# Attention scores of one head at a time, keys split over the two row halves of the array

## The chip, the cores and the metric

The kernel runs on one core of a Trainium2 chip. The metric is the device time of one launch in microseconds (us), from the first to the last instruction with what lies around them; the table below has the median of three runs.

## What is computed

Attention with a bias that a small network computes from positions, and a mixture of two experts out of eight on its result:

```
scores = q @ k.T / 8 + bias[h, i, j]        # B=4, H=8, S=576, D=64
attn   = exp(scores - max) / (sum + 1e-9)
x      = (attn @ v) as 2304 tokens x 512
noisy  = x @ w_gate + log1p(exp(x @ w_noise)) * noise
out    = sum over the top 2 experts: weight * relu(x @ w1[e]) @ w2[e]   # 8 experts, 512 -> 1024 -> 512
```

The bias is relu(psi * w1 + b1) @ w2 with psi = log1p|i-j| / log1p(max(i,1)); it is the same for all batches.

## The kernel before

The program has three stages. First the **bias stage** writes the bias of all heads (36 blocks; `bias_ops`: relus on VectorE and ScalarE at L341 and L344, products at L352, evacuation to a tile X at L360 and L362, a DMA into the bias tiles). Then the **attention stage** runs 16 units, each a batch and a pair of heads, with the routing of a finished batch (`route_ops`) between units. Last the **expert stage** runs the experts (L905, L934); it takes over half of the time and isn't touched.

A unit has four tiles of 128 queries and one (t = 4) that holds the last 64 queries of both heads: nine score tiles of 128 x 576. For each (`pair_ops`):

- *scores*: products on TensorE (PE) into a PSUM tile D of two banks, 288 keys in each (`fqk`, L448). q and k are split into a high and a low part (QH, QL, KH, KL) and three products are summed. The operands' 64 channels fill half of the array's rows; two products in two row halves run side by side. Before, head 0 lies in the upper half and head 1 in the lower, so the two heads of a pair run together and both D tiles must be free. For t = 4 the two heads' queries are stacked with zeros beside them and go through the full array, six products of 128 rows.
- *bias and maximum*: one VectorE instruction per head reads D and the bias and writes a tile E of 128 x 640 (L457, `fttr`); a small copy (L470, `cp`) moves the last 64 keys of head 0 beside those of head 1.
- *exponentials* on ScalarE in place (L463, `fexp`), which also sum up the row.
- *turning*: transposes on PE from E to a D tile, 8 for head 0 and 10 for head 1 (`fturn`, L478), also in row halves, and an evacuation of 512 or 640 columns into ET by VectorE or ScalarE (`evac_op`, L424, L426).
- *values*: ET times v in column halves, 256 or 320 wide, per two or three tiles (`av_ops`, L514), 20 instructions in the trace, and its evacuation into R.

Each unit's q and k are loaded (SyncE's queue, SP) into raw tiles, the high part is cast on VectorE or ScalarE (`fhi`, L405 and L407), and the low part is a subtraction on GpSimd or VectorE (`flo`, L410), a unit ahead, into one of two sets of QH, QL, KH, KL.

The order of everything up to the expert stage is made when the program is built: `Sched` holds operations with a wanted time (`pr`, from constants such as `STEP`, `PO`, `AVO`), costs in a planner's model, dependencies and rings of buffers (`rings`: four D, eight E, two ET, three VT), and puts each on an engine in the order in which it could start. Engines then run their rows in that order and wait for each other by semaphores. Routing has its own operations in the same order: gate products, turned results, token rows to DRAM (x, L707 and L717), ranks, and scatters of slots by GpSimd (L687); after the routing of batch 2 the first tokens of the experts are gathered (L853) and transposed (L871) between the last attention work.

Of the kernel before, what the change touches and what calls it, by code (L numbers as in the profile page):

```python
# [6 lines left out]
F32 = mybir.dt.float32  # L7
# [10 lines left out]
HP = H // 2  # L18
# [3 lines left out]
QW = (EW, S)  # L22
# [46 lines left out]
class Sched:  # L69
# [112 lines left out]
DRAIN, WEIGHTS = 0.18, 0.1  # L182


def build(tc, qs, ks, vp, pe_w1, pe_b1, pe_w2, gate, noise, w1, w2, out):
# [111 lines left out]
    def tw_rest(e):  # L297
# [90 lines left out]
    def unit_ops(u, pr):  # L388
# [4 lines left out]
        for j in (1, 0):  # L393
            if u:
                raw = Buf(f"Q{j}")
                ld = [sd.add(pr - QO[1] + 4 * (1 - j), [[("SP", 0.06), ("DMA", 1.64)]],
                             lambda e, j=j, raw=raw: sy.dma_start(raw.t, (qs, ks)[j][b, hp]), [], [raw], f"ld{u}.{j}")]
            else:
                raw, ld = Buf(f"Q{j}"), []
                raw.slot, raw.t, rings[f"Q{j}"].slots[0] = 0, raws[u, j], None  # L400
# [10 lines left out]
            q = pr - QO[0] + (0.5 if j == 0 else 0)  # L411
# [9 lines left out]
    def evac_op(pr, w, o, i, deps, bufs, kind):  # L421
# [5 lines left out]
        a, d = {640: (0.68, 0.8), 512: (0.55, 0.65), 256: (0.264, 0.331), 128: (0.2, 0.198), 64: (0.17, 0.131)}[w]  # L427
# [4 lines left out]
    def pair_ops(n):  # L432
# [764 lines left out]
```

## Time and profile before

| what | value |
|---|---|
| median of three runs | 764.07 us (763.04 to 764.13) |
| the profiled execution | 764.54 us, of which the span of its instructions is 762.8 us |
| granted TensorE clock over the span | 0.995 |
| PE (matmul) busy | 729.0 us, 96% |
| PE weight loads (PEld) busy | 598.2 us, 78% |
| VectorE (DVE) busy | 472.2 us, 62% |
| ScalarE (ACT) busy | 412.2 us, 54% |
| GpSimd (POOL) busy | 222.4 us, 29% |

The bias stage's last product starts in the 71st microsecond, the attention's last value product ends at about 303 us, and the expert stage fills the rest. A line of the page or of an answer names the line of the code, the engine, the operation, out<-in by the names of the tiles, and times. Busy time of PE is modelled from the starts of matmuls, which are pipelined, so it contains short stalls.

### The profile page before, as it was taken

To read this page: it belongs to the slowest core of one execution; us is meant where nothing else is said; L and a number is where in the kernel's file an instruction comes from. 1 tells how busy PE (TensorE), PEld (TensorE's weight loads), DVE (VectorE), ACT (ScalarE), POOL (GpSimd) and SP (SyncE) were. 2 spreads that over 40 slices of the span, in tenths; PEclk is the share of its full clock that TensorE was granted. 3 is DMA by queue.
4 is the path that set the end of the run, shared out by engine and by line. 5 is a ranking of instruction groups with operands and counts; after the bars stand their busy time and mean duration, and the time that the engine had idled before them with its cause. 6 is when DMAs were issued, how large, how long until landed. Compare 5 with 4: busy or idle time off the path is not lost.

```text
span 762.8 us, 16211 instructions
## 1 busy us (share of the span) xinstructions
PE 729.0 (96%) x6289; PEld 598.2 (78%) x6289; DVE 472.2 (62%) x1104; ACT 412.2 (54%) x815; POOL 222.4 (29%) x229
## 2 busy tenths in 40 slices
PE   6889999999999999999999999999999999999993
PEld 3455677777777775889999899899889889999982
DVE  8898678978977976666543474435344444453361
ACT  8999778897897887334422263332333323333230
POOL 2200122332241242745140435226035034032031
PEclk9999999999999999999999999999999999999998
DMA  5857543432342314458552576355155245345140
GB/s 149 211 160 206 178 149 108 131 90 69 108 91 69 107 23 160 173 145 292 170 202 65 191 240 199 121 169 201 64 172 189 97 153 176 110 138 185 56 143 22
DMA packets 45990, 108.38 MB, mean 142 GB/s; under 512 B 10509, under 2 KB 15373, under 8 KB 45904
## 3 DMA queue, kind: packets, MB, share of 16 engines
q1 hardware_dynamic: 35520, 77.58, 33.5%
q0 software_dynamic: 10384, 29.67, 11.9%
q8 instruction: 52, 0.85, 0.5%
q14 instruction: 34, 0.28, 0.1%
HBM read 77.54 MB, written 19.38 MB: 127 GB/s over the span
## 4 chain that ended last, share of the span: by engine, by line
PE 82%; DVE 10%; ACT 3%; DMA 2%; issue 2%; POOLq 0%; POOL 0%; SPq 0%; DVEq 0%; ACTq 0%
PE Y L934 28%; PE Ha L905 14%; PE Hb L905 14%; PE D L514 9%; PE D L448 7%; PE D L478 4%; PE D L352 3%; DMA bias<-X 2%; DVE E L457 2%; DVE ET L426 2%; PE XT L871 1%; DVE X L717 1%; ACT E L463 1%; DVE lz L627 1%; ACT R L341 1%
## 5 line engine op out<-in xcount | busy, mean ns | idle before, releaser
L934 PE MATMUL Y<-wh,hh 128*128 128x512 f32 x608 | 199.8, 393 | 0.4 <-DVE hh L911 0.3
L934 PEld LDWEIGHTS Y<-wh,hh 128*128 128x128 f32 x608 | 112.8, 186 | 23.6 <-DVE hh L911 0.9
L934 PE MATMUL Y<-wl,hh 128*128 128x512 f32 (+2 forms) x320 | 125.5, 392 | 0.0
L463 ACT ACTIVATE E<-E,mxt 128x576 f32<-128x576 f32 x144 | 110.4, 770 | 7.2 <-DVE mxt L457 6.4
L831 DVE TENSOR_TENSOR wl<-wr,wh 128x1024 fp32r<-128x1024 f32 x77 | 95.4, 1240 | 28.3 <-ACT wh L829 28.2
L457 DVE CUSTOM_DVE_ANT_0 E<-D,bias 128x576 f32<-128x576 f32 x128 | 92.4, 753 | 11.7 <-PE D L448 11.3
L907 ACT ACTIVATE hh<-Ha 128x300 fp32r<-128x300 f32 (+5 forms) x64 | 26.8, 419 | 131.1 <-PE Ha L905 112.5
L514 PE MATMUL D<-ET,vt 128*64 128x256 f32 (+1 forms) x640 | 85.2, 411 | 0.0
L829 ACT ACTIVATE wh<-wr 128x1024 fp32r<-128x1024 f32 x80 | 84.0, 1052 | 1.5 <-DMA wr<-in_w_dram 1.5
L911 DVE SCALAR_TENSOR_TENSOR hh<-Ha,hh 128x128 fp32r<-128x128 f32 (+5 forms) x72 | 30.4, 432 | 84.4 <-ACT hh L907 84.1
L905 PE MATMUL Ha<-xh,wh 128*128 128x300 f32 (+5 forms) x256 | 79.6, 311 | 0.0
L905 PE MATMUL Ha<-xh,wl 128*128 128x300 f32 (+5 forms) x256 | 77.5, 303 | 0.0
L905 PE MATMUL Ha<-xl,wh 128*128 128x300 f32 (+5 forms) x256 | 77.4, 302 | 0.0
L478 PEld LDWEIGHTS D<-identr,E 64*128 64x128 f32 x1312 | 53.8, 138 | 28.6 <-ACT E L463 14.9
L905 PE MATMUL Hb<-xh,wh 128*128 128x300 f32 (+5 forms) x248 | 75.2, 303 | 0.0
L905 PE MATMUL Hb<-xh,wl 128*128 128x300 f32 (+5 forms) x248 | 74.6, 301 | 0.0
L905 PE MATMUL Hb<-xl,wh 128*128 128x300 f32 (+5 forms) x248 | 74.5, 301 | 0.0
L448 PE MATMUL D<-KH,QH 64*128 64x288 f32 (+1 forms) x288 | 70.1, 340 | 4.3 <-DVE mxt L457 2.0
L424 ACT ACTIVATE ET<-D 128x512 f32<-128x512 f32 (+2 forms) x125 | 66.6, 538 | 12.3 <-PE D L478 5.5
L946 POOL DMA_INDIRECT out_dram<-y,ixt x40 | 46.0, 1151 | 86.6 <-DVE y L939 80.6
L478 PE MATMUL D<-identr,E 64*128 64x64 f32 x1312 | 64.9, 229 | 5.9 <-ACT E L463 1.8
L911 DVE SCALAR_TENSOR_TENSOR hh<-Hb,hh 128x224 fp32r<-128x224 f32 (+5 forms) x86 | 30.3, 376 | 62.3 <-ACT hh L907 62.0
(193 smaller groups left out, 1395.4 us busy)
## 6 DMA issues: line engine op xcount, KB each, us to landing
wr<-in_w_dram SPq DMA_DIRECT2D x80, 512.0 KB, 4.6
bias<-X SPq DMA_DIRECT2D x32, 288.0 KB, 3.9
raw<-in_qs_dram SPq DMA_DIRECT2D x16, 320.0 KB, 3.2
vt<-in_vp_dram SPq DMA_DIRECT2D x16, 320.0 KB, 3.4
raw<-in_ks_dram SPq DMA_DIRECT2D x16, 288.0 KB, 3.0
out_dram<-gmz SPq DMA_DIRECT2D x18, 256.0 KB, 3.4
xs_scratch<-X SPq DMA_DIRECT2D x16, 256.0 KB, 2.9
biasr<-X SPq DMA_DIRECT2D x8, 144.0 KB, 2.5
```

What stands on the lines that cost most here:

```text
L424: sc.activation(o(), i(), AF.Copy)
L448: te.matmul(SS[s].t[:, h, :SH], qb.t[x][r, cs], qb.t[y][r, ks], start=(i == 0), stop=(i == 2), skip_group_check=True)
L457: dv.tensor_tensor_reduce(EE[s].t[:, :S].rearrange("p (a b) -> p a b", a=2), SS[s].t[:, :, :SH], bt.rearrange("p (a b) -> p a b", a=2), op ...
L463: sc.activation(EE[s].t[:, :S], EE[s].t[:, :S], AF.Exp, bias=mx[s], scale=-1.0, accum_out=col)
L478: te.transpose(PP[s].t[:, r.start // 64, 64 * k:64 * k + 64], EE[s].t[r, c0:c0 + 128], ident[r, r])
L514: te.matmul(o.t[64 * s:64 * s + 64, 0, :w], vt.t[:, k0, 64 * s:64 * s + 64], et.t[:, 4 * s + k0 if k0 < 4 else 8, :w], start=(k0 == 0), st ...
L829: sc.activation(wh[:, cs], r[:, cs], AF.Copy)
L831: eng.tensor_tensor(wl[:, cs], r[:, cs], wh[:, cs].bitcast(F32), op=OP.subtract)
L905: te.matmul(p[:, :w], a[:, o:o + 128], x[it][:, d, cs], start=(i == 0), stop=(i == 11))
L911: dv.scalar_tensor_tensor(o, p[:, i:i + n], 0.0, HH[:, c0 + i:c0 + i + n].bitcast(F32), op0=OP.max, op1=OP.subtract)
L934: te.matmul(Y if fold else Y[:m], h, w[:, o:o + 512], start=(f == 0 and i == 0), stop=(f == NFC - 1 and i == len(terms) - 1))
L946: st = gp.indirect_dma_start(out=out, out_offset=bass.IndirectOffsetOnAxis(ap=IX[it][:m, 1, k:k + 1], axis=0), in_=y[:m], in_offset=None, ...
```

## The change

Scores are now made for one head at a time. Each head's queries are held in both row halves (`qs` has an array per head, the 64 channels twice), and its keys are split over them: the upper half takes keys 0 to 287, the lower half keys 288 to 575, into the two banks of one D tile. An operation `qk` is six products of one head instead of twelve of two, and needs one free D tile. For t = 4 the two heads' six products each are summed into one D tile, with zeros in the queries of the other head; nothing of the scores goes through the full array. There are two q arrays to load, cast and subtract in each unit instead of one; the E ring has five tiles instead of eight, VT two instead of three, X five instead of four. The planner's costs and wanted times are changed throughout (a price between row products and row transposes, `TURN`, among them), so the order of all engines up to the expert stage is new.

```diff
-QW = (EW, S)
-            c += DRAIN if op.form != self.form else WEIGHTS if t > self.free[e] + WEIGHTS else 0.0
+            c += TURN.get(self.form + op.form, DRAIN) if op.form != self.form else WEIGHTS if t > self.free[e] + WEIGHTS else 0.0
...
-T0, TE, STEP = 15.737, 4.119, 1.527
+T0, TE, STEP = 28.874, 3.875, 1.28
...
+TURN = dict(rowrowt=0.05, rowtrow=0.1)
...
-    for j in (1, 0):
+    for j in (2, 0, 1):
...
-        E=Ring(8, lambda k: (wk if k < 5 else wq).tile([128, EW], F32, name=f"E{k}", bufs=1)),
+        E=Ring(5, lambda k: wk.tile([128, EW], F32, name=f"E{k}", bufs=1)),
...
-        VT=Ring(3, lambda k: wk.tile([128, 5, 128], F32, name=f"vt{k}", bufs=1)),
-        Q0=Ring(1, lambda k: wq.tile([128, EW], F32, name="raw0", bufs=1)),
-        Q1=Ring(1, lambda k: wq.tile([128, S], F32, name="raw1", bufs=1)),
-        QK=Ring(2, lambda k: [wq.tile([128, QW[x[0] == "K"]], F32R, name=f"{x}{k}", bufs=1)
-                                for x in ("QH", "QL", "KH", "KL")]),
+        VT=Ring(2, lambda k: wk.tile([128, 5, 128], F32, name=f"vt{k}", bufs=1)),
+        Q=Ring(2, lambda k: wq.tile([128, EW], F32, name=f"raw{k}", bufs=1)),
+        K=Ring(1, lambda k: wq.tile([128, S], F32, name="raw2", bufs=1)),
+        QK=Ring(2, lambda k: [wq.tile([128, S if x[0] == "K" else EW], F32R, name=f"{x}{k}", bufs=1)
+                              for x in ("QH0_", "QL0_", "QH1_", "QL1_", "KH", "KL")]),
...
-        a, d = {640: (0.68, 0.8), 512: (0.55, 0.65), 256: (0.264, 0.331), 128: (0.2, 0.198), 64: (0.17, 0.131)}[w]
+        a, d = {640: (0.585, 0.735), 512: (0.49, 0.6), 256: (0.27, 0.341), 64: (0.17, 0.131)}[w]
...
-        def fqk(e):
-            for h in range(2):
-                ks = slice(h * SH, h * SH + SH)
-                for i, (x, y) in enumerate(((0, 2), (0, 3), (1, 2))):
-                    for s in range(ns):
-                        r, cs = (HALF[s], slice(128 * t, 128 * t + 128)) if t < 4 else (slice(0, 128), slice(512, EW))
-                        te.matmul(SS[s].t[:, h, :SH], qb.t[x][r, cs], qb.t[y][r, ks], start=(i == 0), stop=(i == 2),
-                                  skip_group_check=True)
-        q = sd.add(pr, ("PE", 0.82), fqk, PREP[u] + QKOP[-1:], [qb] + SS, f"qk{n}", "row" if t < 4 else "full")
+        def fqk(s):
+            def f(e):
+                for h in ((s,) if t < 4 else (0, 1)):
+                    for i, (x, y) in enumerate(((0, 4), (0, 5), (1, 4))):
+                        for r in range(2):
+                            te.matmul(SS[s].t[:, r, :SH], qb.t[2 * h + x][HALF[r], 128 * t:128 * t + 128],
+                                      qb.t[y][HALF[r], h * SH:h * SH + SH], start=(i == 0 and (t < 4 or h == 0)),
+                                      stop=(i == 2 and (t < 4 or h == 1)), skip_group_check=True)
+            return f
+        for s in range(ns):
+            qs_.append(sd.add(pr + STEP * s, ("PE", 0.395 if t < 4 else 0.79), fqk(s), PREP[u][:2 + s if t < 4 else 3] + QKOP[-1:],
+                              [qb, SS[s]], f"qk{n}.{s}", "row"))
...
-    qs = np.zeros((B, HP, 2 * D, EW), f)
+    qs = np.zeros((B, HP, 2, 2, D, EW), f)
+    ks = np.zeros((B, HP, 2, D, 2, SH), f)
```

How the order changes is shown at three places.

**PE, the scores of the last 64 queries in a unit soon after the bias stage.** L448 (before) and L450 (after) are scores from KH, KL and QH, QL, L478 and L485 are transposes of an E tile; a number behind a name tells the buffer. Before:

```order
L478 MATMUL D3_1956<-identr_140,E6_1898 128x64 x8
L478 MATMUL D2_1968<-identr_140,E7_1907 128x64 x10
L448 MATMUL D1_1987<-KH0_1655,QH0_1653 128x288
L448 MATMUL D1_1987<-KL0_1656,QH0_1653 128x288
L448 MATMUL D1_1987<-KH0_1655,QL0_1654 128x288
L448 MATMUL D1_1987<-KH0_1655,QH0_1653 128x288
L448 MATMUL D1_1987<-KL0_1656,QH0_1653 128x288
L448 MATMUL D1_1987<-KH0_1655,QL0_1654 128x288
L478 MATMUL D3_1996<-identr_140,E0_1965 128x64 x8
```

After, where x2 is the two row halves, and QH0 and QH1 are the two heads:

```order
L485 MATMUL D3_2013<-identr_142,E3_1929 128x64 x8
L450 MATMUL D1_2026<-KH0_1686,QH0_0_1682 128x288 x2
L450 MATMUL D1_2026<-KL0_1687,QH0_0_1682 128x288 x2
L450 MATMUL D1_2026<-KH0_1686,QL0_0_1683 128x288 x2
L450 MATMUL D1_2026<-KH0_1686,QH1_0_1684 128x288 x2
L450 MATMUL D1_2026<-KL0_1687,QH1_0_1684 128x288 x2
L450 MATMUL D1_2026<-KH0_1686,QL1_0_1685 128x288 x2
L485 MATMUL D2_2045<-identr_142,E4_1953 128x64 x10
L450 MATMUL D0_2060<-KH0_1686,QH0_0_1682 128x288 x2
L450 MATMUL D0_2060<-KL0_1687,QH0_0_1682 128x288 x2
L450 MATMUL D0_2060<-KH0_1686,QL0_0_1683 128x288 x2
L485 MATMUL D3_2068<-identr_142,E0_2000 128x64 x8
```

The 18 transposes of two heads that followed each other before, and the scores of a whole pair, are now cut into turns of one head's scores and one head's transposes; t = 4 is twelve half products (the six rows on D1_2026) instead of six full ones. The transposes that follow a head's scores belong, here as in nearly all of the program, to the head three before it.

**ACT in the same part of the program.** L463 and L470 are exponentials, L424 and L427 evacuations into ET (turned exponentials) and R (values), L407 a cast. Before:

```order
L407 ACTIVATE KH1_1903<-raw1_1688 128x576
L463 ACTIVATE E6_1898,SM_542<-E6_1898,mxt_1899 128x576
L463 ACTIVATE E7_1907,SM_542<-E7_1907,mxt_1908 128x576
L424 ACTIVATE R0_1934<-D0_1886 128x256
L424 ACTIVATE ET0_1838<-D3_1913 128x4x128
L424 ACTIVATE ET1_1979<-D3_1956 128x4x128
L463 ACTIVATE E0_1965,SM_542<-E0_1965,mxt_1966 128x576
L463 ACTIVATE E1_1981,SM_542<-E1_1981,mxt_1982 128x576
L424 ACTIVATE ET1_1979<-D3_1996 128x4x128
L463 ACTIVATE E2_2006,SM_542<-E2_2006,mxt_2007 128x576
L463 ACTIVATE E3_2037,SM_542<-E3_2037,mxt_2038 128x576
```

After:

```order
L470 ACTIVATE E1_1884,SM_405<-E1_1884,mxt_1885 128x576
L427 ACTIVATE ET0_1894<-D1_1918 128x5x128
L470 ACTIVATE E2_1905,SM_405<-E2_1905,mxt_1906 128x576
L470 ACTIVATE E3_1929,SM_1134<-E3_1929,mxt_1930 128x576
L427 ACTIVATE R0_1968<-D0_1940 128x256
L427 ACTIVATE ET0_1894<-D3_1970 128x4x128
L470 ACTIVATE E4_1953,SM_1134<-E4_1953,mxt_1954 128x576
L427 ACTIVATE ET0_1894<-D2_1987 128x5x128
L427 ACTIVATE ET1_2039<-D3_2013 128x4x128
L470 ACTIVATE E0_2000,SM_1134<-E0_2000,mxt_2001 128x576
L427 ACTIVATE ET1_2039<-D2_2045 128x5x128
```

Evacuations of 640 columns (128x5x128), of which VectorE has 25 of 64 before, all but one stand on ACT now, between the exponentials.

**PE at the end of the attention.** L514 and L520 are the last value products, L871 and L877 the transposes of the experts' first tokens, which need gathered rows xg. Before:

```order
L478 MATMUL D0_5318<-identr_140,E4_5266 128x64 x8
L871 MATMUL Y0_5388<-identr_140,xg_5361 128x128 x4
L478 MATMUL D1_5393<-identr_140,E2_5269 128x64 x10
L514 MATMUL D0_5405<-ET1_5211,vt0_4748 64x256 x10
L478 MATMUL D1_5423<-identr_140,E3_5327 128x64 x8
L871 MATMUL Y1_5434<-identr_140,xg_5361 128x128 x4
L478 MATMUL D0_5442<-identr_140,E1_5331 128x64 x10
L871 MATMUL Y2_5454<-identr_140,xg_5361 128x128 x4
L514 MATMUL D1_5462<-ET0_5314,vt0_4748 64x320 x10
```

After:

```order
L485 MATMUL D1_5511<-identr_142,E2_5458 128x64 x8
L520 MATMUL D0_5579<-ET1_5367,vt1_5190 64x256 x10
L485 MATMUL D1_5592<-identr_142,E4_5461 128x64 x10
L485 MATMUL D0_5605<-identr_142,E0_5499 128x64 x8
L877 MATMUL Y0_5618<-identr_142,xg_5552 128x128 x4
L877 MATMUL Y1_5626<-identr_142,xg_5552 128x128 x4
L877 MATMUL Y2_5631<-identr_142,xg_5552 128x128 x4
L485 MATMUL D1_5638<-identr_142,E1_5520 128x64 x10
L520 MATMUL D0_5657<-ET0_5509,vt1_5190 64x320 x10
```

The three groups of token transposes, spread between the last heads before, stand in one piece now, ahead of the last head's transposes and its value product.

## Rows read from the trace of the kernel before

**Rows 1.** The page, part 1: busy us, share of the span, instructions.

```profile
PE 729.0 (96%) x6289; PEld 598.2 (78%) x6289; DVE 472.2 (62%) x1104; ACT 412.2 (54%) x815; POOL 222.4 (29%) x229
```

**Rows 2.** Two stretches: length, busy us by engine, PE clock, DMA share, GB/s.

```profile
0.00:71.00 71.00, 59.41 (x718) 31.48 (x718) 66.01 (x166) 66.72 (x107) 9.67 (x22) 1.00 0.68 180
71.00:303.00 232.00, 223.26 (x2915) 165.63 (x2913) 185.54 (x565) 191.32 (x455) 66.55 (x57) 1.00 0.37 108
```

**Rows 3.** The chain that ended last, 100 to 300 us: start, us, what.

```profile
154.81 2.84 PE D L514 x20
169.13 2.84 PE D L514 x20
...
182.94 2.87 PE D L514 x20
200.28 2.87 PE D L514 x20
```

**Rows 4.** The timeline from 164 us: start, us, engine, line, [idle before <-releaser].

```profile
163.42 1.56 POOL L410 TENSOR_TENSOR QL<-raw,QH 128x640 fp32r<-128x640 f32 x1
...
164.19 0.78 PE L478 MATMUL D<-identr,E 64*128 64x64 f32 x18
...
164.77 0.41 PE L448 MATMUL D<-KH,QH 64*128 64x288 f32 x2
...
164.99 0.32 PE L448 MATMUL D<-KL,QH 64*128 64x288 f32 x2
...
165.51 0.33 PE L448 MATMUL D<-KH,QL 64*128 64x288 f32 x2
...
165.65 0.82 PE L478 MATMUL D<-identr,E 64*128 64x64 f32 x18
165.84 0.76 DVE L457 CUSTOM_DVE_ANT_0 E<-D,bias 128x576 f32<-128x576 f32 x1 [0.81 <-PE D L448]
...
166.66 0.40 PE L448 MATMUL D<-KH,QH 128*128 128x288 f32 x1 [0.20 <-DVE mxt L457]
166.67 0.77 ACT L463 ACTIVATE E<-E,mxt 128x576 f32<-128x576 f32 x1
...
167.66 0.47 PE L478 MATMUL D<-identr,E 64*128 64x64 f32 x8
...
167.93 0.54 PE L448 MATMUL D<-KH,QH 64*128 64x288 f32 x2
```

**Rows 5.** Waits, 71 to 303 us: who <- for whom: us, times, longest.

```profile
PEld D L478 <- ACT E L463: 11.7, 31, 0.6
...
PEld D L478 <- ACT ET L424: 4.4, 14, 0.5
...
PEld D L448 <- DVE mxt L457: 4.3, 13, 0.5
...
PE D L448 <- DVE mxt L457: 2.0, 9, 0.3
```

**Rows 6.** Groups by shape, 71 to 303 us: count | busy us, mean ns | idle before.

```profile
L424 ACT ACTIVATE ET<-D 128x512 f32<-128x512 f32 x53 | 31.4, 592 | 6.4 <-PE D L478 4.7 <-PE D L514 1.1
L424 ACT ACTIVATE ET<-D 128x640 f32<-128x640 f32 x38 | 26.5, 697 | 0.9 <-PE D L478 0.8
...
L426 DVE COPY ET<-D 128x640 f32<-128x640 f32 x22 | 18.0, 820 | 0.6
```

**Rows 7.** Line L470, 80 to 300 us: ns min/median/max.

```profile
L470 DVE COPY E<-E x58: 173/194/679, 85.7 to 295.3; 128x64 f32<-128x64 f32 x58
```

**Rows 8.** The timeline at the end of the attention, PE and POOL.

```profile
279.81 0.18 PE L730 MATMUL D<-cm,ones 128*128 128x8 bf16 x1
...
288.32 0.96 POOL L853 DMA_INDIRECT xg<-xs_scratch,ixt  x1 [0.30 <-issue]
...
295.00 0.53 PE L871 MATMUL Y<-identr,xg 128*128 128x128 f32 x4 [1.17 <-DVE mxt L457]
```

**Rows 9.** DMA issues: queue, operation, count, median us to landing.

```profile
xg<-xs_scratch,ixt POOLq DMA_INDIRECT x40, 3.8
```

More of the change, by code (lines that the diff above doesn't have):

```diff
@@ L229, in build @@
     sy.dma_start(pw2, pe_w2)
-    for j in (1, 0):
-        raws[0, j] = wq.tile([128, QW[j]], F32, name=f"raw{j}", bufs=1)
-        sy.dma_start(raws[0, j], (qs, ks)[j][0, 0])
+    for j in (2, 0, 1):
+        raws[j] = wq.tile([128, S if j == 2 else EW], F32, name=f"raw{j}", bufs=1)
+        sy.dma_start(raws[j], ks[0, 0] if j == 2 else qs[0, 0, j])
     gw = cst.tile([128, HP, 32], F32)
@@ L392, in unit_ops @@
         PREP[u] = []
-        for j in (1, 0):
+        for j in (2, 0, 1):
+            raw = Buf("K" if j == 2 else "Q")
             if u:
-                raw = Buf(f"Q{j}")
-                ld = [sd.add(pr - QO[1] + 4 * (1 - j), [[("SP", 0.06), ("DMA", 1.64)]],
-                             lambda e, j=j, raw=raw: sy.dma_start(raw.t, (qs, ks)[j][b, hp]), [], [raw], f"ld{u}.{j}")]
-            else:
-                raw, ld = Buf(f"Q{j}"), []
-                raw.slot, raw.t, rings[f"Q{j}"].slots[0] = 0, raws[u, j], None
+                ld = [sd.add(pr - QO[1] + 4 * (j != 2), [[("SP", 0.06), ("DMA", 1.64)]],
+                             lambda e, j=j, raw=raw: sy.dma_start(raw.t, ks[b, hp] if j == 2 else qs[b, hp, j]), [], [raw],
+                             f"ld{u}.{j}")]
+            else:
+                ld = []
+                raw.slot, raw.t = j % 2, raws[j]
+                rings[raw.ring].slots[j % 2] = None
             X, Y = 2 * j, 2 * j + 1
@@ L465, in pair_ops @@
             ps = pr + STEP * s
-            ttr = sd.add(ps + PO[0], ("DVE", 0.677), fttr, [q] + BD[t], [SS[s], EE[s]], f"ttr{n}.{s}")
+            ttr = sd.add(ps + PO[0], ("DVE", 0.677), fttr, [qs_[s]] + BD[t], [SS[s], EE[s]], f"ttr{n}.{s}")
             TTRS.append(ttr)
@@ L485, in pair_ops @@
                 nk = 4 + s
-                tr = sd.add(pr + STEP * s + PO[2], ("PE", 0.06 * nk), fturn(s, nk), [exs[s]] + ([cp] if s else []),
-                            [EE[s], PP[s]], f"T{n}.{s}", "row")
+                tr = sd.add(pr + STEP * s + PO[2], ("PE", 0.059 * nk), fturn(s, nk), [exs[s]] + ([cp] if s else []),
+                            [EE[s], PP[s]], f"T{n}.{s}", "rowt")
                 ETD[u, c].append(evac_op(
@@ L492, in pair_ops @@
         else:
-            tr = sd.add(pr + PO[2], ("PE", 0.3), fturn(0, 5), exs, [EE[0], PP[0]], f"T{n}", "row")
+            tr = sd.add(pr + PO[2], ("PE", 0.295), fturn(0, 5), exs, [EE[0], PP[0]], f"T{n}", "rowt")
             ETD[u, c].append(evac_op(pr + PO[3], 512, lambda: et.t[:, 0:8, 256:320].rearrange("p (r k) q -> p k r q", r=2),
@@ L498, in pair_ops @@
                                          lambda r=r: PP[0].t[64:128, r, 256:320], [tr], [PP[0], et], f"ue{n}.{r}"))
-        if n + 5 == len(tiles):
-            q.f = lambda e, g=q.f: (g(e), [rings["E"].close(k) for k in range(5, 8)])
         if n + 2 == len(tiles):
+            q = qs_[1]
             q.f = lambda e, g=q.f: (g(e), [rings["D"].close(k) for k in range(2, 4)])
@@ L516, in f @@
                               skip_group_check=True)
-        av = sd.add(pr + AVO, ("PE", 2.17 if c == 0 else 2.7), f, ETD[u, c] + [VLD[u]], [et, vt, o], f"av{u}.{c}", "half")
+        av = sd.add(pr + AVO, ("PE", 2.1 if c == 0 else 2.62), f, ETD[u, c] + [VLD[u]], [et, vt, o], f"av{u}.{c}", "half")
         AVQ.append((len(QKOP) - 1 + AVK, av))
@@ L782, in route_ops @@
         for i in range(3, 5):
-            go(f"x{i}", [("PE", 0.24), ("DVE", 0.69), ("SP", 0.06), ("DMA", 0.73)], ["r"], [Buf("D"), Buf("X")], True, "row", [(0, 1)])
+            go(f"x{i}", [("PE", 0.29), ("DVE", 0.6), ("SP", 0.06), ("DMA", 0.73)], ["r"], [Buf("D"), Buf("X")], True, "rowt", [(0, 1)])
         if b == B - 2:
@@ L992, in build @@
                 if t == 0:
-                    QKOP[-1].deps.append(c2)
+                    QKOP[-2].deps.append(c2)
         if b < B - 1:
@@ L1016, in build @@
     sw = sd.add(PT[-1] + 1, [[("SP", 0.06), ("DMA", 0.3), ("Pool", 4.5)]], switch, [o for b in range(B - 1) for o in RDONE[b]], [], "switch")
-    sw.when = lambda: rings["E"].gone >= {5, 6, 7} and rings["D"].gone >= {2, 3}
-    sw.after = TTRS + [o for o in sd.ops if o is not sw and any(b.ring in ("QK", "Q0", "Q1") for b in o.bufs)]
+    sw.when = lambda: rings["D"].gone >= {2, 3}
+    sw.after = TTRS + [o for o in sd.ops if o is not sw and any(b.ring in ("QK", "Q", "K") for b in o.bufs)]
     for k in range(EB):
```

37 lines of the change are left out of this document (21 added, 16 removed).

## Prediction, made before the changed kernel ran

> **What bounds the kernel now.** I read the page first, then two stretches, then the waits and the timeline inside the second one. PE is busy 96% of the span and no other engine over 78% [rows 1]. The stretches show where the change can act: 71 us of bias stage, in which VectorE and ScalarE are busy 66 and 67 us and PE 59; 232 us of attention, with PE at 223.3, ScalarE at 191.3 and VectorE at 185.5 [rows 2]; the rest is experts, which the change doesn't touch. So the attention stretch decides, and in it PE comes first. Two value products of neighbouring units start 14.32 and 13.81 us apart where no batch is routed between them, and 17.34 us where one is [rows 3].
>
> By busy time PE has only 232.0 - 223.3 = 8.7 us of idle to give there. The timeline says that this is too little: matmuls are pipelined, and a stall is hidden in the length that is printed. Products of two halves start every 0.13 us (four pairs from 164.99 to 165.51). Eighteen transposes took 0.58 us to the next start and eight took 0.27, so one costs 0.031 and a stretch of them 0.02 more. But the eighteen at 165.65 were followed by the full-array scores only at 166.66, 1.01 us later, because the VectorE read of the D tile wasn't done [rows 4]. The waits put a sum on that: transposes' weight loads waited 11.7 us for exponentials and 4.4 for evacuations, scores 4.3 (loads) and 2.0 (products) for VectorE's reads, 22.4 us together [rows 5]. That is the pool from which this change can draw.
>
> [...] If one went by matmul busy time all the same, at most 8.7 us of waits could be won, and the sum below would end at about 761 us instead of 757; the waits in the rows speak for the larger pool.
>
> **The change, part by part.** The sum is made against the profiled execution, 764.54 us, which lies 0.47 us above the median of the runs.
>
> *Score streaming: 0.* Each head's tile costs three pairs of half products either way: six pairs for two heads, now three and three. For t = 4, six full products at 0.13 (0.78 us) become six pairs at 0.13. Transposes and value products are the same in number.
>
> *More passages between scores and transposes: +6.2 us.* Counted in the order after the last bias product, passages from transposes to scores go from 66 to 108, and from scores to transposes from 45 to 98: some 47.5 more round trips. One costs: 18 transposes and six pairs took 165.65 - 164.19 = 1.46 us, against 18 x 0.031 + 6 x 0.13 = 1.34, so 0.12 to 0.13 [rows 4]. 47.5 x 0.13 = 6.2.
>
> *No full-array scores: -2.0 us.* The six full products took 167.66 - 166.66 = 1.00 us to the next transposes, 0.22 over their streaming, and the way in 1.01 - 0.58 = 0.43, of which 0.20 at least is a wait that I count below [rows 4]. Without waits that is some 0.25 per tile against 0.13 for a round trip in row form: 16 x 0.12 = 1.9.
>
> *Waits of PE: -13.4 us.* Before, a score operation needed two free D tiles and its two heads passed VectorE and ScalarE one behind the other. In the rows the last pair starts at 165.51 and VectorE reads at 165.84; the first head's exponential ends at 167.44, 1.93 us after, and the second's some 0.77 later [rows 4]. After the change, a head's transposes stand exactly three heads behind its scores in 129 of 144 places. Between lie three tiles of scores (3 x 0.39), three groups of transposes (3 x 0.28) and three round trips (0.39), 2.4 us, and a value product of up to 2.84 in about half of the cases [rows 3]. So 2.4 stand against 1.93 with idle engines: the wait mostly goes, but 0.5 us is a thin margin with ScalarE as full as it gets below. The ends are all 22.4 kept and all gone. Adding up one unit without routing from the new order, with those durations, I find ScalarE late for about one transposes group before each value product, some 0.3 us, twice a unit; 15 units (134 tiles of scores behind the bias stage, nine to a unit) x 0.6 = 9 us stay. 22.4 - 9.0 = 13.4 go.
>
> *ScalarE and VectorE: 0, if ScalarE keeps up.* In the order after the bias stage, evacuations of 640 columns on ScalarE go from 38 to 60 and those of 512 from 53 to 64, at 0.70 and 0.59 us [rows 6]: 15.3 + 6.5, less seven casts that leave (some 4.7) and the overlap of starts with ends (0.1 each), or about +17 us. 191.3 + 17 = 208 us of a stretch of 225 is 93%. VectorE loses 22 copies at 0.82 (18.0) [rows 6] and some of 512, and gains 21 casts of some 0.45: about -13. The cover is ScalarE's 24 us of idle in 232; what it costs if that fails is the first rival.
>
> *A second q per unit: 0.* Sixteen loads, casts and subtractions more. The subtractions (13 on GpSimd at 1.56) [rows 4] add 20 us to 67 in 232 [rows 2], and are made a unit ahead. SP has three raw loads a unit in place of two, ahead of v loads and token stores; a v load now waits for the value product two units back, which is over 13 us before its use. DMA is busy for 0.37 of the stretch [rows 2]. VectorE's small copies take up to 679 ns against a least of 173 [rows 7]; such a delay for ten or so casts and copies more would be 5 us of VectorE, covered by its 46 us of idle. Uncovered, the first scores of a unit would wait, at most some 3 us in a few units: bound +5, below 0 nothing, since nothing gets shorter; I take 0.
>
> *The bias stage: 0.* Up to its last evacuation the order holds the same 144 relus, 36 evacuations and ten VectorE reads of scores; two more q casts stand against two exponentials fewer and two evacuations that move to VectorE. The bound is 1 us either way.
>
> *The end of the attention: +1.3 us.* From the small product of the last routing (L730, 279.81) to the end of the third gather's issue (289.28) are 9.5 us [rows 8], and a gather lands a median 3.8 after its issue begins [rows 9], 288.32 + 3.8 = 292.1, so 12.3 in all. The first token transposes waited 1.17 us at 295.00, for a D tile [rows 8]. In the new order only some 9.2 us of PE work lie between that product and all three groups of token transposes, which stand in one piece with the last value product behind. A wait of some 2.5 us takes the place of the 1.17; the bounds are none (-1.2) and 3.1 (+1.9).
>
> Sum: 764.54 + 6.2 - 2.0 - 13.4 + 1.3 = 756.6 us. Against the median that is 7.4 us less; I say 757.0.
>
> **Rivals.**
> *ScalarE becomes the bound (slower).* If, during the value products, ScalarE runs out of exponentials and then falls behind, its idle time sets the stretch. It had 40.7 us of idle before. With 208 us of work, the stretch gets longer than before as soon as idle exceeds 24 us; if it only falls to 28, the stretch is 236 and the kernel 764.5 + 4 = 768.5 us. For it: 29 value products with at most three heads ahead, five E tiles instead of eight, 63 of 64 large evacuations on ScalarE. Against it: three exponentials of 0.77 cover 2.3 of a value product's 2.84 us. [...]
> *All the waits go.* The pairing was the whole cause: -22.4 + 6.2 - 2.0 + 1.3 gives 747.6. For it: the lag of three heads. Against: ScalarE's 93%.
> *Nothing to measure.* The waits fall by some 5 us and pay the passages: 762.5 to 765.6.
> *The halves of one head don't run side by side.* Then 480 pairs cost 0.13 more, +62 us. The halves write two banks, as the two heads' did; 1 in 100.
>
> **How the numbers follow.** Forecast (750 to 762.5) 0.52, all waits gone (under 750) 0.10, nothing to measure 0.13, ScalarE bound 0.24, halves in turn 0.01. About 0.2%, 1.5 us, is what can be told from no change: faster 0.62, same 0.13, slower 0.25. The range from 748 to 768.5 leaves out half of the second case and about half of the ScalarE case, some 0.17.
>
> **What would show it.** In the changed profile: the waits of transposes for exponentials (11.7) should fall to under 6 and those of scores for VectorE to under 3; value products of units without routing should start 13.3 to 13.7 us apart; ScalarE should be busy for over 90% of the attention stretch and VectorE for under 80%; the bias stage should end at 71 us, and token transposes should show a wait of 2 to 3 us. I am wrong if ScalarE's idle stays over 24 us, or if the weight loads of scores wait for GpSimd's low parts.

## The result, and the profile after

The changed kernel took **753.77 us** (median of 4, 751.81 to 755.81) beside 764.10 us of the kernel before on the same chip: a ratio of 0.987, with a 95% interval of 0.9858 to 0.9883. It is faster by 10.3 us; forecast were 7 (757.0 us, range 748 to 768.5). Run again later, it took 753.82 beside 763.68 (0.9867, 0.9851 to 0.9884). The profiled execution of the changed kernel is the longest of its four, and the other three show a granted clock of 0.990 to 0.993 over the span where it shows 0.988, so the pieces below may hold more time at a low clock than the median does.

The spans of the two profiled executions, 762.8 and 754.0 us, can be cut at three starts on PE, all read from the timelines:

| piece | before | after | difference | forecast |
|---|---|---|---|---|
| to the last product of the bias stage | 70.6 | 68.4 | -2.2 | 0 |
| from there to the last scores (attention) | 222.7 | 210.2 | -12.5 | -9.2 (+6.2 - 2.0 - 13.4) |
| from there to the first expert product (tail) | 13.0 | 18.4 | +5.4 | +1.3 |
| experts | 456.5 | 457.0 | +0.5 | 0 |

So the attention gave more than was forecast, and the tail took back some of it. First the page and the two stretches, in the columns of [rows 1, 2]:

```profile
PE 720.0 (95%) x6385; PEld 589.8 (78%) x6385; DVE 466.6 (62%) x1093; ACT 425.0 (56%) x845; POOL 246.6 (33%) x242
```

```profile
0.00:71.00 71.00, 58.85 (x750) 30.06 (x752) 67.75 (x171) 67.62 (x109) 12.93 (x24) 1.00 0.75 196
71.00:292.00 221.00, 213.45 (x2967) 158.19 (x2969) 178.90 (x549) 203.46 (x483) 85.35 (x68) 0.98 0.45 132
```

ScalarE is busy for 203.46 of 221 us, 92%, where it was 191.3 of 232; VectorE for 81%, where under 80% were forecast. An evacuation group of ScalarE, beside [rows 6], shows why: 60 of the 640 columns, as the order said.

```profile
L427 ACT ACTIVATE ET<-D 128x640 f32<-128x640 f32 x60 | 41.9, 698 | 1.8 <-PE D L485 1.5
```

The waits of PE from 71 to 293 us (who <- for whom: us, times, longest), beside [rows 5]; L450 is the scores, L485 the transposes:

```profile
PEld D L485 <- ACT E L470: 9.2, 22, 0.6
...
PEld D L485 <- ACT ET L427: 1.6, 8, 0.3
```

```profile
PE Y L877 <- DMA xg<-xs_scratch,ixt: 3.2, 1, 3.2
PE D L450 <- POOL QL L413: 0.9, 1, 0.9
...
PE D L450 <- DVE mxt L464: 0.4, 1, 0.4
```

The four waits of [rows 5] summed to 22.4 us. The transposes' for exponentials fell from 11.7 to 9.2, those for evacuations from 4.4 to 1.6, and the scores' for VectorE from 6.3 to 0.8 (0.4 for loads, not among the lines shown, and 0.4 for products): 11.6 are left. A new one stands among them, 3.2 us for the third gather. In both sums the waits of the products lie inside those of their loads (at 166.66 us the load waited 0.34 us and the product 0.20 for the same read), so counted once they are 20.4 and 11.2 us.

Which scores waited for VectorE before shows when the shapes are kept apart (before, 71 to 303 us). The groups of 128*128 are the t = 4 tiles:

```profile
L448 PE MATMUL D<-KH,QH 128*128 128x288 f32 x32 | 11.1, 348 | 1.8 <-DVE mxt L457 1.7
```

```profile
L448 PEld LDWEIGHTS D<-KH,QH 64*128 64x128 f32 x236 | 35.0, 186 | 5.4 <-DVE ET L426 1.6 <-DVE mxt L457 1.4 <-DVE X L717 0.5
...
L448 PEld LDWEIGHTS D<-KH,QH 128*128 128x128 f32 x32 | 6.0, 187 | 3.5 <-DVE mxt L457 2.8 <-ACT R L424 0.2
```

So 4.5 of the 6.3 us (1.7 and 2.8) stood at the t = 4 tiles, whose scores need one free D tile and not two. The pairs, which need two, waited 1.7 us for VectorE's reads.

A turn between scores and transposes, as it now looks (timeline of PE; start, us, line):

```profile
277.96 0.47 PE L485 MATMUL D<-identr,E 64*128 64x64 f32 x10
278.24 0.38 PE L450 MATMUL D<-KH,QH 64*128 64x288 f32 x2
278.46 0.29 PE L450 MATMUL D<-KL,QH 64*128 64x288 f32 x2
278.58 0.30 PE L450 MATMUL D<-KH,QL 64*128 64x288 f32 x2
278.72 0.41 PE L485 MATMUL D<-identr,E 64*128 64x64 f32 x8
```

Three pairs take 278.72 - 278.24 = 0.48 us to the next start, 0.09 over 3 x 0.13; ten transposes take 0.28, 0.03 under 10 x 0.031. Nothing waits.

Adding up the time from each start of PE in the attention piece to the next, by what the start begins, shows where its 12.5 us went; a wait is counted with the work ahead of it. Value products took 77.3 us before and after. Scores, the full-array ones among them, went from 79.9 to 80.7 (+0.8), in 128 stretches of products instead of 72. Transposes of exponentials went from 52.1 to 42.6 (-9.5), the same 1204 records. Transposes of token rows in the routing (L707, now L713) went from 6.8 to 4.0 (-2.8), and what else the routing has gave 1.0.

The end of the attention (PE, with [idle before <-releaser]), beside [rows 8]:

```profile
279.74 2.38 PE L520 MATMUL D<-ET,vt 128*64 128x256 f32 x20 [0.62 <-DVE mxt L464]
...
286.25 1.94 PE L877 MATMUL Y<-identr,xg 128*128 128x128 f32 x12 [3.18 <-DMA xg<-xs_scratch,ixt]
...
288.85 5.35 PE L520 MATMUL D<-ET,vt 128*64 128x320 f32 x20
294.93 1.18 PE L598 MATMUL TP<-R,gw 128*32 128x288 f32 x16 [0.73 <-ACT R L427]
```

Cut at the changes of the granted clock (columns of [rows 2]; the clock is the third from the end):

```profile
278.60:285.50 6.90, 3.82 (x52) 2.44 (x48) 2.00 (x6) 5.59 (x12) 3.18 (x4) 1.00 0.95 357
285.50:292.30 6.80, 5.96 (x32) 3.57 (x34) 2.49 (x4) 3.11 (x5) 2.76 (x3) 0.50 0.13 52
```

PE stood for 3.18 us, and for 6.8 us from 285.5 on the granted clock was 0.50. The twenty value products, 2.91 us in the timeline elsewhere, took 5.35 there.

### The profile page after: what moved, and what is told of

It reads as the page before. It is cut to its first block, busy times and chain, and to the rows that moved or that the text cites. A ratio compares the mean times of both kernels' runs of the same rounds, so it can differ in the third digit from the quotient of the medians.

```text
span 754.0 us, 16550 instructions
## 1 busy us (share of the span) xinstructions
PE 720.0 (95%) x6385; PEld 589.8 (78%) x6385; DVE 466.6 (62%) x1093; ACT 425.0 (56%) x845; POOL 246.6 (33%) x242
## 4 chain that ended last, share of the span: by engine, by line
PE 73%; DVE 9%; issue 7%; ACT 6%; DMA 2%; POOL 1%; SPq 0%; POOLq 0%; ACTq 0%; DVEq 0%
PE Y L940 27%; PE Ha L911 14%; PE Hb L911 13%; PE D L520 6%; PE D L450 4%; DVE E L464 4%; PE D L353 3%; PE D L485 3%; ACT E L470 3%; ACT ET L427 1%; PE XT L877 1%; DMA xg<-xs_scratch,ixt 1%; DVE E L477 1%; POOL slot_list L693 1%; DMA wr<-in_w_dram 1%
## 5 line engine op out<-in xcount | busy, mean ns | idle before, releaser
L470 ACT ACTIVATE E<-E,mxt 128x576 f32<-128x576 f32 x144 | 110.6, 773 | 2.9 <-DVE mxt L464 2.8
L464 DVE CUSTOM_DVE_ANT_0 E<-D,bias 128x576 f32<-128x576 f32 x128 | 94.0, 753 | 3.6 <-PE D L450 2.8
L427 ACT ACTIVATE ET<-D 128x512 f32<-128x512 f32 (+2 forms) x160 | 89.1, 568 | 5.3 <-PE D L485 2.0
L520 PE MATMUL D<-ET,vt 128*64 128x256 f32 (+1 forms) x640 | 87.0, 415 | 0.7 <-DVE mxt L464 0.6
L917 DVE SCALAR_TENSOR_TENSOR hh<-Ha,hh 128x128 fp32r<-128x128 f32 (+5 forms) x72 | 30.4, 432 | 84.2 <-ACT hh L913 83.9
L911 PE MATMUL Ha<-xh,wl 128*128 128x300 f32 (+5 forms) x256 | 77.3, 302 | 0.0
L911 PE MATMUL Ha<-xl,wh 128*128 128x300 f32 (+5 forms) x256 | 77.3, 302 | 0.0
L485 PEld LDWEIGHTS D<-identr,E 64*128 64x128 f32 x1312 | 57.5, 140 | 22.5 <-ACT E L470 13.9
L485 PE MATMUL D<-identr,E 64*128 64x64 f32 x1312 | 67.3, 228 | 3.7 <-ACT E L470 2.5
L520 PEld LDWEIGHTS D<-ET,vt 128*64 128x64 f32 x640 | 43.8, 138 | 32.9 <-issue 5.4
```

Of the source, the lines that this page charges most:

```text
L427: sc.activation(o(), i(), AF.Copy)
L464: dv.tensor_tensor_reduce(EE[s].t[:, :S].rearrange("p (a b) -> p a b", a=2), SS[s].t[:, :, :SH], bt.rearrange("p (a b) -> p a b", a=2), op ...
L470: sc.activation(EE[s].t[:, :S], EE[s].t[:, :S], AF.Exp, bias=mx[s], scale=-1.0, accum_out=col)
L485: te.transpose(PP[s].t[:, r.start // 64, 64 * k:64 * k + 64], EE[s].t[r, c0:c0 + 128], ident[r, r])
L520: te.matmul(o.t[64 * s:64 * s + 64, 0, :w], vt.t[:, k0, 64 * s:64 * s + 64], et.t[:, 4 * s + k0 if k0 < 4 else 8, :w], start=(k0 == 0), st ...
L911: te.matmul(p[:, :w], a[:, o:o + 128], x[it][:, d, cs], start=(i == 0), stop=(i == 11))
```

## The experiments

The theory was that the smaller unit of work (one head's scores, one free D tile) takes the waits of scores and transposes away; its rivals, that ScalarE is the bound, that the planner's new numbers do it, or that the full array's share was the larger. The first four kernels (e) ran in one job, in which the kernel before took 792.4 us: in e1 and e3 some 6 and 9 us were lost once in each of three batches, while GpSimd issued the slot scatters. These four are read by the pieces between such places and by their ratios; three of the edits ran again later, and the table holds the later runs, beside a kernel before of 763.7 (f) and 763.6 us (g).

| run | edit | us | ratio (95%) | attention | scores wait for VectorE | tail |
|---|---|---|---|---|---|---|
| before | | 763.6 | 1 | 222.7 | 6.3 | 13.0 |
| after | | 753.8 | 0.9867 (0.9851 to 0.9884) | 210.2 | 0.8 | 18.4 |
| f1 | both heads in one operation | 774.8 | 1.0153 (1.0134 to 1.0171) | 226.0 | 10.9 | 16.8 |
| f2 | 640 columns dearer on ScalarE | 772.9 | 1.0124 (1.0106 to 1.0141) | 225.4 | 6.3 | 18.9 |
| g2 | old numbers | 772.8 | 1.0117 (1.0101 to 1.0132) | 226.2 | 9.5 | 16.5 |
| g3 | four E tiles | 767.1 | 1.0046 (1.0031 to 1.0062) | 222.7 | 9.6 | 16.9 |
| g4 | t = 4 through the full array | 758.2, one run | | 214.8 | 0.6 | 17.0 |
| f3 | token transposes last, two low parts on VectorE | 751.1 | 0.9850 (0.9827 to 0.9874) | 211.1 | 0.8 | 12.3 |
| g1 | token transposes last | 749.8 | 0.9809 (0.9795 to 0.9823) | 210.1 | 0.8 | 12.3 |

Attention and tail are the pieces of the first table, of the profiled execution; the waits are those of L450 and its loads for L464.

**Both heads in one operation again.** The operands stay as they are in the changed kernel, only the operation is that of a pair:

```diff
-        for s in range(ns):
-            qs_.append(sd.add(pr + STEP * s, ("PE", 0.395 if t < 4 else 0.79), fqk(s), ...
+        q = sd.add(pr, ("PE", 0.79), lambda e: [fqk(s)(e) for s in range(ns)], PREP[u] + QKOP[-1:], [qb] + SS, f"qk{n}", "row")
+        for s in range(ns):
+            qs_.append(q)
```

> The changed kernel with one thing undone: the scores of both heads of a pair are one operation again (twelve half products, two free D tiles at once); keys stay split over the halves, the planner's numbers stay new. Passages from scores to transposes go from 102 to 45 behind the bias stage. Theory A, one head at a time took the waits away: 6 us of passages come back, some 13 us of waits return, 759 to 763 us. Rival B, the new numbers of the plan made the gain: 752 to 755 us, or less by the passages saved (748).

> Both heads' scores in one operation again, as e1_pair. Outside of the stretches in which all engines stood still, its units took 13.0, 17.4 and 15.9 us, so a batch should take some 58 to 60 us against 55.9. Theory A (one head at a time took the waits away): 4 to 9 us over the changed kernel. Rival B (the plan's numbers): within 2 us of it.

In the first job it took 792.4 us, 0.9974 (0.9929 to 1.0019). Its periods of nine score tiles are those of f1 where no scatter falls into them (13.03, 17.44 and 15.89 us; f1 has 13.03, 17.45 and 15.89), so f1 decides: 21 us over the changed kernel, where 4 to 9 were expected, and 11 over the kernel before. Of the 18.2 us between the profiled spans 15.8 lie in the attention and 3.5 in the bias stage. Waits of its attention stretch:

```profile
PEld D L485 <- ACT E L470: 8.8, 19, 1.0
...
PEld D L450 <- DVE mxt L464: 6.9, 15, 1.3
...
PEld D L450 <- ACT ET L427: 4.4, 11, 0.6
...
PE D L450 <- DVE mxt L464: 4.0, 8, 1.1
```

The scores' waits for VectorE are back, 10.9 us; the transposes' for exponentials stay (8.8). But what came back is for the most part not a wait for a second free D tile. From 71 us to the last scores, the weight loads of scores waited 14.1 us ahead of the first head's first product and 2.3 ahead of the second head's, for whatever cause. One of the longest of these waits (timeline of f1, DVE and PE):

```profile
150.36 1.11 DVE L408 CAST QH<-raw 128x640 fp32r<-128x640 f32 x2
...
151.07 0.72 PE L485 MATMUL D<-identr,E 64*128 64x64 f32 x18
151.40 0.81 DVE L413 TENSOR_TENSOR QL<-raw,QH 128x640 fp32r<-128x640 f32 x1
152.12 0.74 DVE L464 CUSTOM_DVE_ANT_0 E<-D,bias 128x576 f32<-128x576 f32 x1
...
152.93 0.40 PE L450 MATMUL D<-KH,QH 64*128 64x288 f32 x2 [1.15 <-DVE mxt L464]
...
153.44 0.29 PE L450 MATMUL D<-KH,QH 64*128 64x288 f32 x2
```

Two casts and a subtraction of a q stand ahead of VectorE's read, and the first head's scores wait for it; the second head's, at 153.44, don't wait. And the runs f2, g2 and g3 below keep one head at a time and have 6.3 to 9.6 us of the same wait. So f1 shows that the gain doesn't survive the larger operation under these numbers; which wait the smaller operation removes, and how much of the 21 us is its own, it doesn't show, since the planner made another order for the pair with numbers that fit the single head.

**Evacuations shared again.** ScalarE's planning price for 640 columns goes from 0.585 to 0.985, so that VectorE takes 24 of the 64; PE's order stays, but for a few rows.

```diff
-        a, d = {640: (0.585, 0.735), 512: (0.49, 0.6), 256: (0.27, 0.341), 64: (0.17, 0.131)}[w]
+        a, d = {640: (0.985, 0.735), 512: (0.49, 0.6), 256: (0.27, 0.341), 64: (0.17, 0.131)}[w]
```

> The changed kernel, in which the planner is told a higher ScalarE cost for evacuations of 640 columns: 24 of 64 go to VectorE again (1 in the changed kernel), PE's order stays the same but for some ten rows. ScalarE loses 23 x 0.70 = 16 us, VectorE gains 23 x 0.82 = 19 us. If ScalarE at 92% is what PE waits for: 3 to 6 us less, 748 to 751. If PE's own passages and products are the bound: within 1.5 us, 752.5 to 755.5. If VectorE's reads get late: 756 to 760.

> 24 evacuations of 640 columns on VectorE instead of 1, as e4_evac_dve. If ScalarE is what PE waits for: 3 to 6 us under the changed kernel. If PE's own passages and products are the bound: within 1.5 us. If VectorE's reads of scores stand behind the evacuations and D tiles get free later: 2 to 8 us over it.

It was 19 us slower than the changed kernel, where 2 to 8 were the most expected (in the first job 798.0 us, 1.003, 0.9989 to 1.0071). The stretch of 71 to 292 us, and waits in it:

```profile
71.00:292.00 221.00, 205.34 (x2873) 152.50 (x2871) 183.75 (x553) 182.52 (x436) 91.02 (x69) 0.99 0.42 120
```

```profile
ACT ET L427 <- PE D L485: 16.6, 24, 1.4
...
PEld D L450 <- DVE mxt L464: 4.5, 14, 0.4
```

VectorE and ScalarE are now busy alike, 183.8 and 182.5 us, and ScalarE waits 16.6 us for transposes where it waited 2.0 in the changed kernel. So a fuller use of VectorE was no gain: 21 us of room for ScalarE made nothing shorter. That the copies of 0.82 us, which stand ahead of VectorE's reads of scores, are the cause is argued from the waits; the order is another one here too.

**The numbers alone, and the layout alone.** First the kernel before with the changed kernel's planning numbers, evacuation prices and the price for turning between row products and row transposes; then the changed kernel with the old ones.

```diff
-T0, TE, STEP = 15.737, 4.119, 1.527
+T0, TE, STEP = 28.874, 3.875, 1.28
...
+TURN = dict(rowrowt=0.05, rowtrow=0.1)
```

> The kernel before with nothing but the new planner's numbers (wanted times, costs, the price between row products and transposes; AVK stays 4, since it counts operations). Theory A: within 3 us of the kernel before, 761 to 767. Rival B: most of the gain, 752 to 757.

> The changed kernel's layout and unit of work (one head's scores an operation, its keys split over the halves, five tiles of exponentials) with the numbers by which the order is planned put back to those of the kernel before (due times, evacuation prices, no price for turning between row products and row transposes); TensorE turns between scores and transposes 87 and 105 times instead of 97 and 108. Theory that the unit of work gives the time back: last scores 210 to 216 us after the last bias product, 754 to 760 us, ratio 0.987 to 0.995. Rival, that the numbers do: the stretch stays at the 222 of the kernel before or longer, 763 us or more, ratio 0.999 or more.

The numbers alone gave 816.4 us in the first job, 1.0255 (1.0187 to 1.0323), and weren't run again: neither theory of them (761 to 767 or 752 to 757) held, as far as a run of that job tells. The layout alone gave 772.8, 19 more than the changed kernel and 9 more than the kernel before: my theory of it (754 to 760) fell. Its waits:

```profile
PEld D L485 <- ACT E L470: 13.7, 29, 2.2
PEld D L450 <- DVE mxt L464: 6.3, 16, 0.8
...
PE D L485 <- ACT E L470: 4.0, 9, 2.1
```

PE waits 17.7 us for exponentials. Neither half, as it ran here, brings anything; the gain is of both together. One old number means something else in the new layout, though: `AVK = 4` counts operations of scores ahead of a value product, pairs in the kernel before and single heads in this run, so its value products stand ahead of two heads' scores that they follow in the changed kernel. How the layout would do with old numbers that fit it is open.

**Four E tiles instead of five.**

```diff
-        E=Ring(5, lambda k: wk.tile([128, EW], F32, name=f"E{k}", bufs=1)),
+        E=Ring(4, lambda k: wk.tile([128, EW], F32, name=f"E{k}", bufs=1)),
```

> The changed kernel with four tiles of exponentials instead of five; the order is planned anew under that limit. Theory: each half tile holds its buffer until its transposes are through, so with four VectorE's reads, and with them the scores, are planned later or wait: 3 to 12 us longer than the changed kernel, ratio to the kernel before 0.990 to 1.003, the stretch from last bias product to last scores 213 to 222 us. Rival, that the fifth tile is not needed since a unit of work is now half as large: 752 to 755 us, ratio 0.985 to 0.989.

13 us more than the changed kernel, a little beyond the 3 to 12 expected. The attention piece is as long as before, and the scores wait for VectorE again:

```profile
PEld D L485 <- ACT E L470: 7.0, 17, 0.6
...
PEld D L450 <- DVE mxt L464: 5.6, 11, 0.8
...
PE D L450 <- DVE mxt L464: 4.0, 8, 0.6
```

With this plan five tiles suffice and four cost 13 us. The reads themselves waited only 0.6 us for transposes in this trace, so the theory, that a read can't start where its E tile still waits to be turned, shows at most in the planned order; it wasn't tested apart from that.

**The fifth query tile through the full array.**

```diff
+                if t == 4:
+                    for h in range(2):
+                        for i, (x, y) in enumerate(((0, 4), (0, 5), (1, 4))):
+                            te.matmul(SS[s].t[:, h, :SH], qb.t[x][:, 512:EW], qb.t[y][:, h * SH:h * SH + SH], ...
```

> The changed kernel with the scores of a unit's fifth, narrow query tile taken through the full array again, three products a head as in the kernel before, on operands that are now laid out for halves: the scores of those 64 queries are no longer the right ones, so what comes behind them (the routing above all) is other work, and only the attention stretch is read. Theory that a switch between full array and halves has its price: the stretch from last bias product to last scores 1.5 to 4 us longer than the 210.0 of the changed kernel. Rival, that only the streaming counts, which is the same: 209.5 to 210.7 us.

Only the attention piece is read, 214.8 us against 210.2: 4.6 more, a little over the 1.5 to 4 expected. The full array first (timeline of PE), then the same place in the changed kernel:

```profile
203.04 0.46 PE L491 MATMUL D<-identr,E 64*128 64x64 f32 x8
203.43 0.40 PE L450 MATMUL D<-KH,QH 128*128 128x288 f32 x1
...
204.42 0.53 PE L491 MATMUL D<-identr,E 64*128 64x64 f32 x10
```

```profile
200.61 0.46 PE L485 MATMUL D<-identr,E 64*128 64x64 f32 x8
200.91 0.40 PE L450 MATMUL D<-KH,QH 64*128 64x288 f32 x2
...
201.81 0.47 PE L485 MATMUL D<-identr,E 64*128 64x64 f32 x10
```

Six full products take 0.99 us to the next start and twelve half ones 0.90; the eight transposes ahead take 0.39 and 0.30. That is 0.18 us a tile, 2.9 for sixteen. The other 1.7 lie mostly at the token transposes (5.6 us in place of 4.0), and whether the full array or the new order causes those is open.

**Token transposes last.** They may only follow the last value products:

```diff
-        o = sd.add(PT[-1] + XS + 0.1 * k, ("PE", 0.436), lambda e, k=k: x_split(0, k, "t"), [sw], [], "xs")
+        o = sd.add(PT[-1] + XS + 0.1 * k, ("PE", 0.436), lambda e, k=k: x_split(0, k, "t"), [sw, AVQ[-1][1]], [], "xs")
```

> The changed kernel with the token transposes moved behind the last value product; nothing else moves on PE. In the changed kernel's trace PE waited 3.2 us for the gather, the granted clock halved from 285.5 to 292.3 us, and the last value product took 6.08 us instead of 2.84. If the loss lay in both, wait and clock: the value product covers the gather, the clock stays up, 6 us less, 747 to 749. If the clock falls all the same: 3 us less, about 751. If the expert stage has to wait for the tokens' split instead: no gain, 753 to 755.

> The changed kernel with one edit: the token transposes of the first expert block may only follow the last value products of the last unit. Theory: in the changed kernel TensorE stands 3.2 us for the third gather with work still to do, its granted clock is then 0.5 for 6.8 us, and the remaining products run at that clock; with the products in the wait's place both go. First expert product 12 to 13 us after the last scores instead of 18.3, time 747.0 to 748.5, ratio to the kernel before 0.978 to 0.980; everything ahead of the last scores as in the changed kernel, tiles 18 to 27 in 15.2 us. Rival: the clock falls or the gather is waited for anyway, a little later: 751.5 to 754, ratio 0.984 to 0.987.

In the first job 778.8 us, 0.9811 (0.9733 to 0.9889); then 749.8, 0.9809 (0.9795 to 0.9823). That is 4 us below the changed kernel by the medians and 5.6 by the spans (748.4 against 754.0), a little above the 747.0 to 748.5 expected, and the best version of all that ran. The same place as above:

```profile
283.33 0.52 PE L485 MATMUL D<-identr,E 64*128 64x64 f32 x10 [0.31 <-ACT ET L427]
...
284.77 2.90 PE L520 MATMUL D<-ET,vt 128*64 128x320 f32 x18 [0.20 <-DVE ET L429]
287.61 1.21 PE L877 MATMUL Y<-identr,xg 128*128 128x128 f32 x12
```

No wait for the gather, no fall of the clock (eighteen value products take 2.90 us), and 12.3 us of tail instead of 18.4: the 5.4 us that the tail had cost, and 0.7 more.

**Low parts of one unit on VectorE.** In the changed kernel scores waited 0.91 us for GpSimd's low part in the third unit, and the granted clock was 0.50 for 3.4 us right after, from 84.2. The edit stands beside the one above:

```diff
-            PREP[u].append(sd.add(q + 0.1, LO, flo, [hi], [raw, qb], f"lo{u}.{j}"))
+            PREP[u].append(sd.add(q + 0.1, LO[1:] if u == 2 and j < 2 else LO, flo, [hi], [raw, qb], f"lo{u}.{j}"))
```

> The changed kernel with two edits: the token transposes behind the last value product (as e3_tail_last), and both low parts of the queries of unit 2 on VectorE, since PE waited 0.9 us for GpSimd's at 82 us and the granted clock fell to half for 3.4 us just after. If the clock follows PE's stalls there and at the end: about 6 us from the end and 2 us from unit 2, 0.976 to 0.979 of the kernel before. If the clock falls anyway: 3 to 4 us in all, 0.982.

It took 751.1, some 1.3 us more than g1 without it, the intervals of the ratios just part (0.9827 and 0.9823), and both expectations (0.976 to 0.979, 0.982) were missed. The wait moved and didn't go; the clock was low for 6.8 us from 82.9 on, where g1 has 3.4 (means of 0.54 and 0.77 from 82.5 to 90 us):

```profile
83.39 0.80 PE L485 MATMUL D<-identr,E 64*128 64x64 f32 x10 [0.71 <-ACT E L470]
```

The subtractions, 1.56 us for two on VectorE, stand ahead of its reads of scores, and the exponentials come 0.71 us late instead.

## Why the prediction was right, point by point

*The range and the sign held, and the waits fell, as forecast. That the time came within 3 us of the forecast is in part luck: passages were priced some 4 us too dear, the waits and the full array were off by some 1 to 2, and the end of the attention, 4 us too cheap, was partly offset by a bias stage 2 us shorter.*

- **Passages, +6.2: too dear.** By the medians of the timelines, a pair of heads took 18 transposes and twelve score products before, 0.587 and 0.903 us to the next start. Now it takes eight, six, ten and six, 0.272, 0.485, 0.279 and 0.485. That is 1.52 us for 1.49, or for the 1.46 of [rows 4]: 0.03 to 0.06 us for the one round trip more, where 0.13 were taken. 47.5 of them are an estimated 1.5 to 2.9 us. The prediction charged each new passage with all that the old stretch of a pair took over its streaming; but eighteen transposes with twelve products paid that too, and a shorter stretch pays less (three pairs 0.485 - 0.39 = 0.095 us over their streaming, six 0.903 - 0.78 = 0.123).
- **No full-array scores, -2.0: a little small.** 0.18 us a tile, -2.9 in all.
- **Waits, -13.4: the direction right, the makeup wrong.** With passages of 1.5 to 2.9 and 2.9 for the full array, the attention piece leaves 11.1 to 12.5 us for them. The four named waits gave 10.8 (22.4 to 11.6, where 9.0 were to be left), or 9.2 counted once: the pool of 22.4 held the products' 2.0 us twice. Scores' waits for VectorE went nearly to nothing (under 3 forecast, 0.8 found), while transposes' for exponentials stayed at 9.2 (under 6 forecast), so the reckoning with "three heads behind" gave too much to the exponentials. Nor was the need for two free D tiles what most of the scores waited for before: 4.5 of their 6.3 us stood at t = 4 tiles, which need one. What took those waits away isn't shown. The remainder, 1.9 to 3.3 us, lies among waits and work that the prediction left out of its pool: the routing's token transposes (-2.8) and its other operations (-1.0) take less time on PE. Starts of value products show where in the program the gain lies, beside [rows 3]; first the chain, then PE's timeline:

```profile
147.81 2.84 PE D L520 x20
161.68 2.84 PE D L520 x20
189.94 2.84 PE D L520 x20
...
203.63 2.84 PE D L520 x20
```

```profile
161.61 2.91 PE L520 MATMUL D<-ET,vt 128*64 128x320 f32 x20
...
174.69 2.91 PE L520 MATMUL D<-ET,vt 128*64 128x320 f32 x20
...
189.88 1.30 PE L520 MATMUL D<-ET,vt 128*64 128x320 f32 x8
```

  Without routing 13.87, 13.08 and 13.69 us lie between neighbours, where 13.3 to 13.7 were forecast and 14.32, 13.81 and 14.1 stood before. With routing it is 15.19 in place of 17.34. Of the 3.8 us that such a batch of four units gains, 2.1 lie in the unit with the routing, a place of which the prediction said nothing.
- **ScalarE, 0: right**, at 92% against the 93% worked out, and f2, with 21 us less on ScalarE, gained nothing. Its rival, given 0.24, was the largest one; its condition (idle over 24 us) wasn't met, with 17.5 us of idle in 221.
- **A second q, 0: right but for one place**, the 0.91 us wait for GpSimd's low part at 82.4, a thing that the prediction had named as a sign of being wrong, and the low clock after it.
- **Bias stage, 0: wrong by 2.2 us.** The piece ends at 68.4 in the changed kernel and in g1, g3 and g4, but at 70.2 in f2 and 72.0 in f1, which have its layout and numbers too (69.3 in e1, the same kernel as f1); at 71.3 with the layout alone, at 71.5 with the numbers alone and at 70.6 before. So layout and numbers together don't make the 68.4 by themselves. In f1 PE stood for 1.84 us ahead of 51.81, and the granted clock was 0.50 for 3.4 us from 52.0. Equal counts of operations had stood for equal time; what in the order does it isn't settled.
- **End of the attention, +1.3: the other mis-sized term, +5.4.** The wait was named and sized well (3.18 us against "some 2.5", bound 3.1). In place of the 1.17 before it makes 2.0 us. What was left out is that the work behind it then ran at a granted clock of 0.50 for 6.8 us, in which PE was busy for 5.96: half of that, an estimated 3.0 us, and the 2.0 are nearly the whole 5.4. g1, with work in the wait's place, returned 6.1 us.
- **Matmul busy time**, the pool of 8.7 us from which one would have arrived at 761, was too small, as the waits had said: attention alone gave 12.5 us.

## What to carry to other kernels

Cutting an operation that asks for two PSUM tiles into two that ask for one can pay, but before that reason is given, look at which product of it waited: here most of the wait stood at tiles that needed only one. Price an added passage by old stretch against new (0.03 to 0.06 us here), and not by all that one stretch takes over its streaming (0.13). Count a stall once, at the load or at its product. A layout and the order planned for it are one change: each half alone was slower here than what stood before, so undoing one part measures a misfit as well as the part. When a wait is put ahead of work that could go first, count the wait and then what the granted clock does to the work behind it (here 2.0 us, and an estimated 3.0 at 0.50).

## What the runs showed of the hardware

- At the end of the attention, the granted TensorE clock fell to 0.50 where PE had stood for the gather: for 6.8 us after 3.18 us without work in the changed kernel and after 3.28 in f2, for 3.4 us after 2.63 in g3 and after 1.54 in f1. In g1, with no stand over 0.62 us there, it did not fall: the last eighteen value products took 2.90 us.
- Shorter stands don't settle it. Around 82 us PE waited 0.37, 0.91 and 0.23 us within 3 us in the changed kernel, and the clock was 0.50 for 3.4 us from 84.2; in g4 it waited 0.38, 0.91 and 0.23 at the same place, and the clock stayed at 1.00.
- Among the waits of PE, that of scores for VectorE went with the length of the attention piece: 0.6 to 0.8 us where the piece is 210 to 215, 6.3 to 10.9 where it is 222 to 226. The transposes' wait for exponentials did not: 9.4 us in the changed kernel, 7.0 with four E tiles, 12.9 in f2, 17.7 in g2. Which of the two, the wait or the length, is the cause in each, these runs don't separate.
- The nine score tiles beside a batch's slot scatters took 22.40 us in e3 and 13.38 in g1, which is the same kernel, on the same chip a quarter of an hour later; the eighteen tiles ahead took 28.65 and 28.64. No run tells the cause.
